# Moving the tiles that TensorE reads to SBUF addresses that are multiples of 512 bytes, in an attention and expert-layer kernel

## The chip, the cores and the metric

The kernel runs on one core of a Trainium2 chip. The metric is device time in microseconds (us), from runs on the chip; a profiled execution has a time of its own beside them, and a span, which is the time from its first instruction to its last.

## What is computed

Eight batches of eight heads. `x` has 512 tokens and `state` 32 rows per head, 64 numbers each. Attention goes both ways between `x` and `state`; the two results are laid one after the other (544 rows in each batch), the heads are joined to rows of 512 numbers, and a layer with a mish activation follows.

```python
scores = scale * np.matmul(x, state.transpose(0, 1, 3, 2))       # 8 x 8 x 512 x 32
a = softmax(scores);   xread = np.matmul(a, state)
scores2 = scale * np.matmul(state, x.transpose(0, 1, 3, 2))      # 8 x 8 x 32 x 512
a2 = softmax(scores2); sread = np.matmul(a2, x)
y = np.concatenate([xread, sread], axis=2)                       # to 4352 x 512
h = y @ w_in                                                     # w_in 512 x 2048
g = h * np.tanh(softplus(h))                                     # mish
out = g @ w_out                                                  # w_out 2048 x 512
```

Weights come as 64-bit floats and are joined to 32-bit ones on the chip; the rest is fp32.

## The kernel before, in words

**Two halves for each factor.** The large products use the type `F32R`. To keep precision, each operand is split in a high and a low part of that type, and each product is three matmuls: high by high, high by low, low by high. So `ah`/`al` are the parts of the attention weights, `swh`/`swl` of state times `w_in`, `gh`/`gl` of the activated hidden layer, and `wo` holds both parts of `w_out`.

**The two big products.** `xread @ w_in` is computed as attention weights times (state times `w_in`): `sw_slice` makes the second factor with small fp32 matmuls into `swp` and splits it. A batch has eight slots; each takes two blocks of 128 hidden columns.

- `gemm1` (the tile `ph`) does 12 matmuls for a slot, each with a weight of 128x128 from `swh` or `swl` and a moving operand of 128x512 from `ah` or `al`. There are 8 batches x 8 slots x 12 = 768.
- `mish` (ScalarE) makes `g` from `ph`; `high_g` and `low_g` (VectorE) split it.
- `gemm2` (the tile `acc`) does 24 matmuls for a slot, each with a weight of 128x128 from `gh` or `gl` and a moving operand of 128x512 from `wo`. There are 8 x 8 x 24 = 1536, and 96 more with the tile `acc_s`.

The 256 rows that come from `state` (`sread`, gathered in `srT_h` and `srT_l`) are multiplied by `w_in` itself in `gemm1_s`, before the last batch: 192 matmuls into `ph_s`, each with a weight of 128x128 from `wh` or `wl` and a moving operand of 128x256 from `srT_h` or `srT_l`.

**Order.** In the first batch each engine's order is written out by hand (the list of steps at L614). After that, the slots run one after another; `gemm2` of a slot comes two slots later (`LAG`), and the attention of the next batch is put beside the slots. All matmuls are issued by helpers, so the profile names one line, L67, for nearly all of them; groups are told apart by their tiles.

**Where tiles lie.** Tiles of a pool are laid one behind the other in each partition of SBUF, in the order in which their tags are first used. The first of the kernel's own is `ident` (L99), at byte 16,512, which is 32 x 512 + 128. It is 512 bytes long, and so are, or multiples of that, all tiles behind it up to the three small softmax tiles `mx`, `s1` and `r1` (L332): 64 bytes each, two buffers of each, 384 bytes in all.

Of the kernel before, what the change touches and what calls it, by code (L numbers as in the profile page):

```python
# [9 lines left out]
F32 = mybir.dt.float32  # L10
# [7 lines left out]
P = 128  # L18
# [56 lines left out]
def state_attention_mish_kernel(ctx, tc, x, state, w_in, w_out, out):  # L75
# [5 lines left out]
    const = ctx.enter_context(tc.tile_pool(name="const", bufs=1))  # L81
    pool = ctx.enter_context(tc.tile_pool(name="pool", bufs=2))
# [4 lines left out]
    def misc(name):  # L87
        return ps_m.tile([P, 512], F32, tag="m", name=name)
# [6 lines left out]
    def temp(name, shape=(P, S)):  # L95
        return pool.tile(list(shape), F32, tag="t", name=name, bufs=5)


    ident = const.tile([P, P], F32, name="ident")  # L99
    make_identity(nc, ident)  # L100

    w_in_sb = const.tile([P, NC, DF], F32, name="w_in_sb")
# [130 lines left out]
    def attention(b, sn, xq=None):  # L233
# [84 lines left out]
        e1, small = {}, {}  # L318

        def wide(a):  # L320
            return a.unsqueeze(2).to_broadcast([P, 16, NS])

        def groups(a):
            return a.rearrange("p (g n) -> p g n", n=NS)

        def transposed(pt, src):
            for t in range(NT):
                last["PE"] = pe.transpose(pt[:, t * P:(t + 1) * P], src[:, t * P:(t + 1) * P], ident)

        def soft1_t(kc):  # L330
            e1[kc] = temp(f"e1_{b}_{kc}")
            small[kc] = [pool.tile([P, 16], F32, tag=n, name=f"{n}_{b}_{kc}") for n in ("mx", "s1", "r1")]  # L332
            if b == 0:
                src = misc(f"scT_{b}_{kc}")
                transposed(src, sc[kc])
            else:
                src = e1[kc]
                dve.transpose(src, sc[kc])
            yield
            mx = small[kc][0]  # L340
            dve.tensor_reduce(mx, groups(src), AX.X, ALU.max)
            dve.tensor_sub(groups(e1[kc]), groups(src), wide(mx))
# [40 lines left out]
        def soft1():  # L383
            whole(*(soft1_t(kc) for kc in two))
            for kc in two:
                soft1_x(kc)
            whole(soft1_n(), *(soft1_a(kc) for kc in two))
# [20 lines left out]
        def sreadT():  # L408
# [8 lines left out]

        own = dict(
            x=x_transposed, st=lambda _: state_blocks(b, sn), sc=lambda _: scores(), tr=soft1_t, ex=soft1_x,
            no=lambda _: soft1_n(), pr=soft1_a, mm=soft2_m, ee=soft2_e, et=e2_transposed, sr=sread,  # L420
            rt=lambda _: sreadT(), fill=fill, aT=aT)
# [229 lines left out]
    for key, j in slots:  # L651
# [15 lines left out]
        n = pending[0][3] // 2  # L667
# [74 lines left out]
```

## Time and profile before

| | us |
|---|---|
| median of 3 runs | 679.45 (678.8 to 679.7) |
| profiled execution, its own time | 678.77 |
| its span | 677.0 |

An engine's busy time is a share of the span. A matmul's duration covers its way through the array, so matmuls that follow each other overlap, and their rate is read from their starts, or from the chain of work that ended last: there the time of a piece is divided by its number of matmuls. "PEld" is the loading of weights, which runs beside matmuls. "PEclk" is the clock that TensorE was granted, in tenths of 2.4 GHz.

### The profile page before, as it was taken

How to read it: one execution, taken by the hardware profiler on the slowest of the kernel's cores; microseconds unless marked ns; L12 is line 12 of the kernel's file. 1: busy time of each engine (PE TensorE's matmuls, PEld its weight loads, DVE VectorE, ACT ScalarE, POOL GpSimd, SP SyncE). 2: the span in 40 equal slices, each digit the busy share in tenths (PEclk: the TensorE clock that was granted, in tenths of full speed). 3: DMA queues.
4: the chain of work that ended last, by engine and by line, in shares of the span. 5: the costliest groups of instructions: out<-in, count | busy, mean ns of one | idle time of the engine just before them, and what ended most of it. 6: DMA issues, size and time to landing. Idle time of an engine off the chain costs nothing.

```text
span 677.0 us, 11013 instructions
## 1 busy us (share of the span) xinstructions
PE 668.7 (99%) x4642; PEld 525.2 (78%) x4642; DVE 339.9 (50%) x520; ACT 263.0 (39%) x418; POOL 0.7 (0%) x6
## 2 busy tenths in 40 slices
PE   8999999999999999999999999999999999999997
PEld 6777777777777777777777877777777789877785
DVE  4878894358328533565327533564427345222221
ACT  4997853245216312541226312632236234122210
POOL 0000000000000000000000000000000000000000
PEclk9999999999999999999999999999999999999999
DMA  9965212401131022302131022202100001000001
GB/s 326 393 232 186 46 19 83 103 7 29 67 74 23 1 63 83 48 1 63 36 74 22 1 63 81 45 0 64 50 14 0 1 1 63 1 17 17 0 1 62
DMA packets 74929, 41.61 MB, mean 61 GB/s; under 512 B 56192, under 2 KB 64384, under 8 KB 74880
## 3 DMA queue, kind: packets, MB, share of 16 engines
q1 hardware_dynamic: 74592, 40.85, 20.6%
q8 instruction: 36, 0.59, 0.4%
q14 instruction: 13, 0.11, 0.0%
q10 hardware_dynamic: 288, 0.07, 0.0%
HBM read 31.98 MB, written 8.91 MB: 60 GB/s over the span
## 4 chain that ended last, share of the span: by engine, by line
PE 90%; DMA 4%; ACT 3%; DVE 2%; issue 1%; SPq 0%; DVEq 0%; ACTq 0%
PE acc L67 51%; PE ph L67 24%; PE swp L67 5%; PE ph_s L67 3%; PE acc_s L67 3%; DMA wir<-in_moe_w_in_dram 2%; PE srp L67 1%; DMA wor<-in_moe_w_out_dram 1%; PE sc L67 1%; ACT L67 1%; PE e2p L67 1%; PE st L67 1%; DVE gl L67 1%; DMA x<-in_x_dram 0%; ACT g L67 0%
## 5 line engine op out<-in xcount | busy, mean ns | idle before, releaser
L67 PE MATMUL acc<-wo,gh 128*128 128x512 f32 x1024 | 326.0, 399 | 0.0
L67 PEld LDWEIGHTS acc<-wo,gh 128*128 128x128 f32 x1024 | 188.8, 188 | 51.8 <-issue 9.8
L67 PE MATMUL acc<-wo,gl 128*128 128x512 f32 x512 | 202.6, 396 | 0.1
L67 ACT ACTIVATE g<-ph 128x512 f32<-128x512 f32 x128 | 74.0, 598 | 210.1 <-DVE gl L67 193.6
L67 PEld LDWEIGHTS acc<-wo,gl 128*128 128x128 f32 x512 | 96.2, 188 | 23.6 <-DVE gl L67 0.8
L67 DVE CAST gh<-g 128x1024 fp32r<-128x1024 f32 x64 | 44.3, 692 | 114.9 <-PE acc L67 106.5
L67 DVE TENSOR_TENSOR swl<-swp,swh 128x512 fp32r<-128x512 f32 (+1 forms) x72 | 43.0, 626 | 95.7 <-ACT swh L67 95.6
L67 DVE TENSOR_TENSOR gl<-g,gh 128x1024 fp32r<-128x1024 f32 x64 | 78.1, 1220 | 4.8 <-DVE gh L67 0.5
L67 PE MATMUL ph<-ah,swh 128*128 128x512 f32 x256 | 79.9, 394 | 0.2 <-ACT g L67 0.2
L67 PE MATMUL ph<-al,swh 128*128 128x512 f32 x256 | 78.9, 390 | 0.0
L67 PE MATMUL ph<-ah,swl 128*128 128x512 f32 x256 | 78.6, 390 | 0.0
L67 PEld LDWEIGHTS ph<-ah,swh 128*128 128x128 f32 x256 | 47.7, 188 | 11.6 <-ACT g L67 0.7
L67 ACT CAST swh<-swp 128x512 fp32r<-128x512 f32 (+1 forms) x72 | 35.3, 546 | 54.0 <-PE swp L67 54.0
L67 PEld LDWEIGHTS ph<-al,swh 128*128 128x128 f32 x256 | 48.1, 188 | 10.5
L67 PEld LDWEIGHTS ph<-ah,swl 128*128 128x128 f32 x256 | 48.1, 188 | 10.3
L67 ACT ACT_TABLE_LOAD x35 | 44.9, 1283 | 16.3 <-DVE sm L67 10.9
L67 PE MATMUL swp<-w_in_sb,bd 64*32 64x256 f32 x1024 | 36.0, 383 | 0.3 <-DVE w_in_sb L67 0.2
L67 DVE STREAM_TRANSPOSE xT<-xq 128x512 f32<-128x512 f32 x24 | 25.5, 1101 | 17.4 <-PE e2p L67 17.3
L67 PEld LDWEIGHTS swp<-w_in_sb,bd 64*32 64x32 f32 x1024 | 15.2, 106 | 16.9 <-issue 12.7
L67 ACT COPY o<-acc 128x512 f32<-128x512 f32 x16 | 9.4, 586 | 48.0 <-PE acc L67 40.4
L67 DVE COPY o<-acc 128x512 f32<-128x512 f32 x16 | 11.1, 691 | 22.6 <-PE acc L67 17.2
L67 PE MATMUL acc_s<-wo,gh_s 128*128 128x512 f32 x64 | 20.2, 396 | 0.0
(76 smaller groups left out, 482.7 us busy)
## 6 DMA issues: line engine op xcount, KB each, us to landing
x<-in_x_dram SPq DMA_DIRECT2D x32, 256.0 KB, 3.9
wir<-in_moe_w_in_dram SPq DMA_DIRECT2D x16, 512.0 KB, 10.1
wor<-in_moe_w_out_dram SPq DMA_DIRECT2D x16, 512.0 KB, 6.9
out_dram<-o SPq DMA_DIRECT2D x32, 256.0 KB, 2.3
xq<-in_x_dram SPq DMA_DIRECT2D x192, 32.0 KB, 2.3
out_dram<-o_s SPq DMA_DIRECT2D x8, 64.0 KB, 1.7
sn<-in_state_dram SPq DMA_DIRECT2D x14, 32.0 KB, 2.0
sn<-in_state_dram ACTq DMA_DIRECT2D x2, 32.0 KB, 3.1
```

Of the source, the lines that this page charges most:

```text
L67: made = method(*args, **kwargs)
```

## The change

```diff
-    ident = const.tile([P, P], F32, name="ident")
+    ident = const.tile([P, 96 + P], F32, name="ident")[:, 96:]
     make_identity(nc, ident)
...
         def soft1_t(kc):
             e1[kc] = temp(f"e1_{b}_{kc}")
-            small[kc] = [pool.tile([P, 16], F32, tag=n, name=f"{n}_{b}_{kc}") for n in ("mx", "s1", "r1")]
+            small[kc] = [
+                pool.tile([P, n], F32, tag=t, name=f"{t}_{b}_{kc}")[:, :16] for t, n in (("mx", 32), ("s1", 16), ("r1", 16))]
```

The identity gets 96 unused floats (384 bytes) in front of it, and each of the two buffers of `mx` gets 64 unused bytes behind its 16 numbers. No instruction is added, removed or moved on any engine: the built programs differ in addresses and line numbers alone. The addresses, from the allocation of the two built programs (a name with several buffers shows the first; their distances are multiples of 512 unless the row says otherwise):

| tile | read by TensorE as | first byte before | past a multiple of 512 | first byte after | past a multiple of 512 |
|---|---|---|---|---|---|
| `ident` | moving, in transposes | 16,512 | 128 | 16,896 | 0 |
| `w_in_sb` | moving of `swp` | 17,024 | 128 | 17,408 | 0 |
| `srT_h`, `srT_l` | moving of `ph_s` | 49,792 | 128 | 50,176 | 0 |
| `wo` (eight tiles) | moving of `acc`, `acc_s` | 57,984 | 128 | 58,368 | 0 |
| `xT`, `e1`, `e2`, `wh`, `wl` (five buffers shared) | `wh`, `wl`: weights of `ph_s` | 149,120 | 128 | 149,504 | 0 |
| `bd` | weights of `swp` (slices 128 bytes apart) | 159,360 | 128 | 159,744 | 0 |
| `mx` | not read | 165,504 | 128 | 165,888 | 0 |
| `ah`, `al` | moving of `ph` | 165,888 | 0 | 166,400 | 0 |
| `swh`, `swl` | weights of `ph` | 182,272 | 0 | 182,784 | 0 |
| `gh`, `gl` | weights of `acc`, `acc_s` | 206,848 | 0 | 207,360 | 0 |
| `srd` | weights of eight transposes | 223,424 | 192 | 223,936 | 192 |

The weights of `ph`, `ph_s`, `acc` and `acc_s` are slices of 512 bytes at multiples of 512 bytes within their tiles. The moving operands of `ph`, `acc` and `acc_s` are 2,048 bytes long, and all begin at a multiple of 2,048 bytes within their tiles; taken by 2,048, `ah` and `al` begin at 0 before and at 512 after, `wo` at 640 before and at 1,024 after.

## Rows read from the trace of the kernel before

**Rows 1.** The page: span, then each engine's busy time; granted clock by slice.
```profile
span 677.0 us, 11013 instructions
...
PE 668.7 (99%) x4642; PEld 525.2 (78%) x4642; DVE 339.9 (50%) x520; ACT 263.0 (39%) x418; POOL 0.7 (0%) x6
...
PEclk9999999999999999999999999999999999999999
```

**Rows 2.** The page: chain that ended last, by engine, then by line.
```profile
PE 90%; DMA 4%; ACT 3%; DVE 2%; issue 1%; SPq 0%; DVEq 0%; ACTq 0%
PE acc L67 51%; PE ph L67 24%; PE swp L67 5%; PE ph_s L67 3%; PE acc_s L67 3%; DMA wir<-in_moe_w_in_dram 2%; PE srp L67 1%; DMA wor<-in_moe_w_out_dram 1%; PE sc L67 1%; ACT L67 1%; PE e2p L67 1%; PE st L67 1%; DVE gl L67 1%; DMA x<-in_x_dram 0%; ACT g L67 0%
```

**Rows 3.** Waits of PE: engine, tile, waited for: us in total, times, longest.
```profile
PE warm L67 <- POOL ident masks.py:199: 1.4, 1, 1.4
PE scT L67 <- ACT scs L67: 0.8, 1, 0.8
...
```

**Rows 4.** Chain that ended last, in order: start us, us, what, number.
```profile
542.73 5.79 PE acc L67 x24
...
551.42 11.50 PE ph_s L67 x96
562.92 5.58 PE acc L67 x24
568.50 5.75 PE ph_s L67 x48
574.25 5.58 PE acc_s L67 x24
...
629.69 5.59 PE acc L67 x24
635.28 2.73 PE ph L67 x12
638.01 2.80 PE acc L67 x12
640.81 1.02 PE swp L67 x32
...
647.57 5.59 PE acc L67 x24
653.17 2.73 PE ph L67 x12
655.90 14.01 PE acc L67 x60
```

**Rows 5.** Busy time of each engine by stretch; then granted clock, DMA share, GB/s.
```profile
23.00:40.00 17.00, 16.64 (x96) 12.60 (x88) 13.55 (x18) 16.90 (x23) 0.00 (x0) 1.00 1.05 388
80.00:100.00 20.00, 19.73 (x124) 14.27 (x123) 19.90 (x34) 11.85 (x19) 0.00 (x0) 1.00 0.17 27
100.00:540.00 440.00, 439.83 (x3100) 343.83 (x3099) 217.00 (x344) 156.27 (x260) 0.00 (x0) 1.00 0.17 42
...
656.00:669.00 13.00, 13.00 (x57) 10.49 (x56) 2.39 (x3) 0.54 (x1) 0.00 (x0) 1.00 0.00 0
```

**Rows 6.** Weight loads by tile: shapes, number, busy us, mean ns of one, idle.
```profile
L67 PEld LDWEIGHTS acc<-wo,gl 128*128 128x128 f32 x512 | 96.2, 188 | 23.6 <-DVE gl L67 0.8
L67 PEld LDWEIGHTS ph<-al,swh 128*128 128x128 f32 x256 | 48.1, 188 | 10.5
...
L67 PEld LDWEIGHTS ph_s<-srT_h,wh 128*128 128x128 f32 x64 | 12.3, 192 | 0.1
```

**Rows 7.** Chain that ended last, its start, same columns.
```profile
0.74 3.07 DMA x<-in_x_dram
...
4.29 7.86 DMA wor<-in_moe_w_out_dram
...
12.16 11.45 DMA wir<-in_moe_w_in_dram
```

## The prediction

> **What bounds the kernel now.** I read first the busy times, then the chain of work that ended last, then who TensorE waited for. TensorE (PE) is busy 99% of the span [rows 1] and holds 90% of the chain [rows 2]. A busy PE could still be a waiting one, so the waits decide: PE waited eight times in the whole execution, once for 1.4 us and once for 0.8 us at the start, and the other six are shorter still [rows 3]. From 100 to 540 us VectorE is busy 217 of 440 us and ScalarE 156, while PE has 439.8 of 440 [rows 5]. So the end is set by how closely matmuls follow each other, and a fraction of a nanosecond per matmul counts, if it holds for hundreds of them. The granted clock is full, 2.4 GHz, in every slice [rows 1], and plays no part.
>
> **At what rate they follow.** In the chain, pieces of one kind of matmul stand with their time and number [rows 4], and the quotient is the spacing:
>
> - `ph`: 2.73 us for 12, 227.5 ns each.
> - `acc`: 5.59 us for 24, 232.9 ns each; the last piece, 14.01 us for 60, gives 233.5 ns. `acc_s` reads the same `wo`: 5.58 for 24, 232.5 ns.
> - `ph_s`, with 256 columns: 11.50 us for 96, 119.8 ns each.
>
> `ph` and `acc` are the same instruction: weights of 128x128, a moving operand of 128x512, both of the same type, six and more of them summed in one bank. Yet `acc` takes 5.4 ns longer each time. It isn't the other engines: in the last piece VectorE is busy 2.39 us of 13 and ScalarE 0.54, no DMA runs [rows 5], and the spacing is the longest of all. What differs is where the operands lie. In `ph` the moving operand (`ah`, `al`) and the weights (`swh`, `swl`) all begin at a multiple of 512 bytes. In `acc` the weights do, and the moving `wo` begins 128 bytes past one.
>
> **What kind of effect it would be.** 512 and 256 columns at 2.4 GHz are 213.3 and 106.7 ns, worked out from the granted clock. So `ph` has 14.2 ns over its columns, `ph_s` 13.1 and `acc` 19.6. `ph_s` has no more than `ph`, although its moving `srT` begins 128 bytes past a multiple of 512. But its weights `wh`, `wl` do so as well. A start that is off for itself would have to show in `ph_s`, at least in part; a start that is off against the other operand would show in `acc` alone, which is what the rows have. While one matmul's 512 columns are read, the weights of the next are read beside them (188 ns of the 233 are weight loading [rows 6]), so two streams out of SBUF run at once and can get in each other's way, or not, by their addresses. There is also a direct sign that starts matter: a weight load takes 188 ns from `gl` and `swh`, which are at a multiple of 512, and 192 ns from `wh`, which is 128 past one, with the same shape [rows 6]. The weights in `ph` and `acc` begin at every multiple of 512, not of 1,024 or 2,048 alone, and the mean of 188 ns leaves no room for a finer rule there.
>
> After the change `wo`, `gh`, `gl`, `ah`, `al`, `swh` and `swl` all begin at multiples of 512: by both readings, absolute and relative, `acc` should have the spacing of `ph`.
>
> **The change part by part.** No instruction is added or moved, so there are only the prices of addresses.
>
> - *`acc` and `acc_s`*, 1536 + 96 = 1632 matmuls. From 232.9 ns to what `ph` has, 227.5 ns, is 5.4 ns. `ph` pieces have heavier company than `acc` (the splitting of `g` on VectorE falls in them), so `acc` may come out a little below; the excess of the last, undisturbed piece over `ph` is 233.5 - 227.5 = 6.0 ns. I take 5.7 ns: 1632 x 5.7 = 9.3 us. With 5.4 it is 8.8, and with 6.0 it is 9.8.
> - *What of it isn't on the path.* The 192 `acc` matmuls of the first batch run beside full engines: ScalarE 16.90 of 17 us from 23 to 40, VectorE 19.90 of 20 from 80 to 100 [rows 5]. There a faster PE meets a later `gl` or `wo`. At most 192 x 5.7 = 1.1 us is lost, at least 0; I take half, 0.55. From 100 us on the other engines are busy half the time, and nothing else is near.
> - *`ph`*, 768 matmuls, moves by 512 bytes and keeps its place by 512. I take 0; the other end is the second rival below.
> - *`ph_s`*, 192 matmuls, weights and moving operand move alike. Its weight loads should go from 192 to 188 ns, which is hidden: the loads overlap each other, since 119.8 ns is shorter than one. I take 0.
> - *The small fp32 matmuls* (`swp` 5% of the chain, `srp`, `sc`, `e2p` 1% each [rows 2], together 8% of 677 us, about 54 us) also get other addresses. A block of `swp` takes 1.02 us for 32 [rows 4]. I take 0, since no row shows one of them at another start; if they changed by the share that `acc` does (5.4 of 232.9, 2.3%), it would be 1.2 us either way.
> - *DMAs, VectorE, ScalarE.* All loads now land at multiples of 512. In the first 24 us they are on the path: 3.07 + 7.86 + 11.45 = 22.4 us [rows 7]. No row shows a load to a multiple of 512, so again 0, bounded by the same 2.3% either way, 0.5 us. VectorE and ScalarE have idle time for what a start may cost them. The setting of `ident` delays nothing: as many bytes are written as before. The Trainium skill (DMA: Bandwidth & Descriptors, "How a descriptor splits into AXI transactions") says that a transfer which doesn't start at a multiple of 256 bytes needs one transaction more; a row of 2,048 bytes at 128 past would take 9 instead of 8. By that page the loads would gain up to a ninth of 22.4 us, 2.5 us as an estimate; no row here shows it.
>
> The sum: 9.3 - 0.55 = 8.75 us less. Against the profiled execution's own time that is 678.77 - 8.75 = 670.0 us; that execution is 0.7 us under the median of the runs, 679.45, and against this it is 670.7 us, the forecast.
>
> **The rivals.**
>
> *Nothing changes, 679.45 us.* The 5.4 ns would then belong to `acc` for another reason: `wo` is read in the order high, low, high, the weight `gh` is used twice in a row, and four banks take turns instead of two. For it speaks that `ph_s`, at 128 past, has as little over its columns as `ph`, so that a plain rule "off a multiple of 512 is slow" is wrong as it stands; against it the 188 and 192 ns, and that I find no mechanism in these three. The Trainium skill also stands on this side: SBUF — State Buffer, "Who interferes with whom", gives TensorE two independent read ports, one for the moving operand and one for weights, and says that it never waits on anyone; by it `acc` and `ph` should run alike already, and the rows (232.9 against 227.5) disagree.
>
> *The boundary of moving operands is 1,024 bytes: 674.8 us.* `wo` then comes right, at 1,024 past a multiple of 2,048, and `ah`, `al`, at 512, go wrong. 768 x 5.4 = 4.1 us come back: 670.7 + 4.1 = 674.8. The trace can't exclude it, because moving `ah` and `al` stand only at multiples of 2,048 in it.
>
> *The boundary is 2,048 bytes: slower, 683.6 us.* The mechanism is the same, and the place is `ph`: `wo` at 1,024 stays as slow as it is, while `ah` and `al` lose the multiple of 2,048 that they had. 679.45 + 4.1 = 683.6. It decides from the point where a moving operand must begin at a multiple of its own length. Against it and the one before: the weights show no difference between multiples of 512, so two streams that meet by their distance can't tell them apart either.
>
> **How the numbers follow.** The forecast, `acc` near `ph`'s spacing, gets 0.76; 1,024 bytes 0.06; nothing 0.11; 2,048 bytes 0.07. Within the forecast, the low end is 9.8 us for `acc` with nothing lost, 1.2 for the small matmuls and 0.5 for the loads: 679.45 - 11.5 = 668.0. Its high end is 8.8 - 1.1 = 7.7 us gained and 1.2 + 0.5 lost elsewhere: 673.5. I widen the range at the top to 676.0, to hold the case of 1,024 bytes, and by half a microsecond at the bottom, to 667.5, since a spacing below that of `ph` can't be excluded; it then holds a little over 0.8. The forecast's own range is 668.0 to 673.5. A measurement of this kernel can tell about 0.2%, 1.4 us, from no change. Faster by more: 0.76 + 0.06 = 0.82; within it 0.11; slower 0.07.
>
> **What would show it.** In the chain of the changed kernel, pieces of 24 `acc` should take 5.4 to 5.5 us instead of 5.59, the last 60 about 13.65 instead of 14.01, and pieces of 12 `ph` still 2.73. `ph_s` stays at 5.75 for 48, with weight loads at 188 instead of 192 ns. If `acc` falls and `ph` rises to 2.80, the boundary is larger than 512. If `acc` falls but the end doesn't follow, waits of PE on VectorE's `gl` will have appeared. If `acc` stays at 232.9, the addresses aren't the reason, and the forecast is wrong at its first step.

## The result: 670.15 us, and the profile after

The changed kernel has a median of 670.15 us (669.92 to 670.25, 4 runs), beside 679.29 us of the kernel before; the ratio is 0.9867, with a 95% interval of 0.9853 to 0.988. The profiled execution took 670.19 us, its span is 668.4 us.

From the page of the changed kernel, span and busy times, as in [rows 1]:

```profile
span 668.4 us, 11013 instructions
...
PE 659.5 (99%) x4642; PEld 525.1 (79%) x4642; DVE 339.1 (51%) x520; ACT 263.0 (39%) x418; POOL 0.7 (0%) x6
```

TensorE (PE) does the same 4642 matmuls in 9.2 us less, and still has 99% of the span. The chain of work that ended last, in order (start us, us, what, number), answers to [rows 4]:

```profile
561.69 5.75 PE ph_s L67 x48
567.44 5.47 PE acc_s L67 x24
...
621.98 5.44 PE acc L67 x24
627.42 2.72 PE ph L67 x12
630.14 2.72 PE acc L67 x12
632.86 1.02 PE swp L67 x32
...
639.55 5.44 PE acc L67 x24
644.99 2.72 PE ph L67 x12
647.71 13.62 PE acc L67 x60
```

24 `acc` matmuls take 5.44 us instead of 5.59, which is 226.7 ns each instead of 232.9; the last 60 take 13.62 us instead of 14.01, 227.0 instead of 233.5. `ph` has 2.72 us for 12, 226.7 ns, so the two products now run alike. `ph_s` and `swp` are as they were.

Summed from start to start over both traces, `acc` and `acc_s` cost 8.1 us less, `ph` 0.9 us less, all the rest 0.4 us more; the last matmul starts 8.7 us earlier.

Almost none of that gain is from the first batch. Two pieces of it in the chain of the kernel before, then a piece and the end of it in that of the changed kernel:

```profile
61.16 1.59 PE acc L67 x6
...
102.78 2.74 PE ph L67 x12
```

```profile
61.16 1.59 PE acc L67 x6
...
87.91 1.14 DVE gl L67
89.04 1.15 DVE wo L67
90.23 1.42 PE acc L67 x5
91.65 1.02 PE swp L67 x32
92.68 4.33 PE acc L67 x18
97.00 2.72 PE ph L67 x12
99.72 2.93 PE acc L67 x12
102.65 2.72 PE ph L67 x12
```

The first matmuls after 90 us follow VectorE's `gl` and `wo`, the short piece of `acc` at 61.16 us takes as long as before, and the `ph` at 102.65 us stood at 102.78 us before: 0.13 us for a whole batch.

### The profile page after: what moved, and what is told of

Read it like the earlier page. It is cut to its first block, busy times and chain, and to the rows that moved or that the text cites. A ratio compares the mean times of both kernels' runs of the same rounds, so it can differ in the third digit from the quotient of the medians.

```text
span 668.4 us, 11013 instructions
## 1 busy us (share of the span) xinstructions
PE 659.5 (99%) x4642; PEld 525.1 (79%) x4642; DVE 339.1 (51%) x520; ACT 263.0 (39%) x418; POOL 0.7 (0%) x6
## 4 chain that ended last, share of the span: by engine, by line
PE 87%; DMA 5%; DVE 4%; ACT 2%; issue 1%; SPq 1%; DVEq 0%; ACTq 0%
PE acc L67 49%; PE ph L67 23%; PE swp L67 4%; PE ph_s L67 3%; PE acc_s L67 3%; DMA wor<-in_moe_w_out_dram 2%; DMA wir<-in_moe_w_in_dram 1%; PE srp L67 1%; DMA x<-in_x_dram 1%; PE sc L67 1%; PE e2p L67 1%; DVE e L67 1%; DVE gl L67 1%; PE st L67 1%; ACT L67 1%
## 5 line engine op out<-in xcount | busy, mean ns | idle before, releaser
L67 PE MATMUL acc<-wo,gh 128*128 128x512 f32 x1024 | 321.2, 395 | 0.2 <-DVE wo L67 0.2
L67 PE MATMUL acc<-wo,gl 128*128 128x512 f32 x512 | 199.9, 390 | 0.1
```

The lines of the kernel that those rows point to most:

```text
L67: made = method(*args, **kwargs)
```

## The experiments

All are the same instructions in the same order, with tiles at other addresses. "At 128" means 128 bytes past a multiple of 512. The theories: A, what counts is the distance between the starts of the moving operand and of the weights; B, the moving operand's own start counts; C, something else.

**All tiles at 128.** The second half of the change alone:

```diff
-    ident = const.tile([P, 96 + P], F32, name="ident")[:, 96:]
+    ident = const.tile([P, P], F32, name="ident")
```

> Only the second half of the change: the small tile is larger, the identity has nothing in front. wo, gh, gl, ah, al, swh, swl, srT, wh, wl then all begin 128 bytes past a multiple of 512. Theory A (what counts is the distance between the starts of the moving operand and of the weights, taken by 512): the distance is 0 everywhere, so acc has 226.7 ns for each matmul, ph too, and the time is that of the changed kernel, 670.2 us, within 1. Theory B (each moving operand must itself begin at a multiple of 512): acc stays at 233 and ph goes from 227.5 to 233, so 679.3 + 768 x 5.4 ns = 683.4 us. Theory C (something else in acc made it slow, and the identity's start or the like cured it): 679 us.

Measured: 670.49 us, ratio to the kernel before 0.9873 (0.9859 to 0.9888), the same as with all tiles at 0. In the chain that ended last:

```profile
622.05 5.44 PE acc L67 x24
627.49 2.72 PE ph L67 x12
...
647.77 13.62 PE acc L67 x60
```

`wo`, `ah` and all their weights are 128 past a multiple of 512, and the pieces of `acc` and `ph` take no longer for it. Theory B falls: none of these tiles has to begin at a multiple of 512, or of 256, for itself.

**The first half alone.** `mx` as before, so `wo` is at 0 and `ah`, `al`, `swh`, `swl`, `gh`, `gl` are at 384:

```diff
-                pool.tile([P, n], F32, tag=t, name=f"{t}_{b}_{kc}")[:, :16] for t, n in (("mx", 32), ("s1", 16), ("r1", 16))]
+                pool.tile([P, n], F32, tag=t, name=f"{t}_{b}_{kc}")[:, :16] for t, n in (("mx", 16), ("s1", 16), ("r1", 16))]
```

> Only the first half of the change: 384 bytes in front of the identity, the small tile as before. wo, srT, wh, wl then begin at a multiple of 512, while ah, al, swh, swl, gh, gl begin 384 bytes past one. Theory A (distance between moving operand and weights): 0 in ph and ph_s, 128 in acc (wo at 0, weights at 384), as in the kernel before, so acc 232.9 ns, ph about 227.5, time 679 us. Theory B (the moving operand's own start): acc 226.7 and ph 233, so 670.2 + 768 x 6 ns = 674.8 us.

Measured: 679.33 us, ratio 1.0001 (0.9991 to 1.001). The chain that ended last:

```profile
630.29 5.59 PE acc L67 x24
635.89 2.73 PE ph L67 x12
...
656.51 14.01 PE acc L67 x60
```

These are the pieces of [rows 4] to the last digit, although every tile lies elsewhere: the distance in `acc` is again 128. Of the two edits, the larger small tile does all of the work, since it brings the distance in `acc` to 0; the bytes in front of the identity, alone, leave the distance in `acc` at 128.

**The distance moved to the other product.** `ah` and `al` alone at 128, all else as in the changed kernel (64 bytes more in each `mx`, and 384 unused bytes behind `al`):

```diff
-... (("mx", 32), ("s1", 16), ("r1", 16))]
+... (("mx", 48), ("s1", 16), ("r1", 16))]
...
             lo = pool.tile([P, S], F32R, tag=f"al{kc}", name=f"al_{b}_{kc}")
+            if b == 0 and kc == 1:
+                pool.tile([P, 96], F32, tag="pad", name="pad", bufs=1)
```

> The changed kernel with ah and al alone (the moving operands of ph) 128 bytes past a multiple of 512; wo and all weights at a multiple of 512. Theory A (distance of moving operand and weights, taken by 256 after the runs with wo at 64 and 256): the slow spacing moves from acc to ph: ph 233 ns (2.80 us for 12), acc 226.7 ns (5.44 us for 24), and 670.2 + 768 x 6.2 ns = 674.9 us. Theory C (the slowness is the wo tile's own, cured by its place): all stays as in the changed kernel, 670 us.

Measured: 675.38 us, ratio 0.9942 (0.9928 to 0.9957). The chain:

```profile
626.96 5.46 PE acc L67 x24
632.41 2.79 PE ph L67 x12
635.21 2.73 PE acc L67 x12
```

Now `ph` is the slow one, 2.79 us for 12 or 232.5 ns, and `acc` runs at 227.5. The slowness goes with the distance, not with the tile, so theory C falls for `wo`, too.

**Other distances of `wo`.** The identity's front and `mx` are sized so that `wo` moves and `ah`, `al` and the weights of both products stay at 0; `srT`, `wh`, `wl` and `w_in_sb` move with `wo` (front, then `mx`, in floats: 32 and 64 for 256 bytes; 112 and 24 for 64; 16 and 72 for 192; 104, 16 and one unused tile of 24 floats in front of `mx` for 32). The first, as a diff against the changed kernel:

```diff
-    ident = const.tile([P, 96 + P], F32, name="ident")[:, 96:]
+    ident = const.tile([P, 32 + P], F32, name="ident")[:, 32:]
...
-... (("mx", 32), ("s1", 16), ("r1", 16))]
+... (("mx", 64), ("s1", 16), ("r1", 16))]
```

> wo, srT, wh, wl, w_in_sb begin 256 bytes past a multiple of 512; ah, al, swh, swl, gh, gl at a multiple of 512. By both theories, a period of 256 bytes would give acc at 226.7 ns and 670 us; with a period of 512 acc stays slow, at 233 ns or more (256 is the farthest that it can be from 0), so 679 us or more: if the extra time grows with the distance, twice 6 ns, 239 ns and 689 us.

Measured: 670.81 us, ratio 0.9876 (0.9861 to 0.989). The chain with `wo` at 256:

```profile
639.58 5.44 PE acc L67 x24
645.02 2.72 PE ph L67 x12
647.74 13.61 PE acc L67 x60
```

A distance of 256 is as good as 0.

> wo, srT, wh, wl, w_in_sb begin 64 bytes past a multiple of 512; ah, al, swh, swl, gh, gl at a multiple of 512. If the extra time grows with the distance: half of that at 128, so 3 ns, acc about 230 ns and 675 us. If every distance that isn't 0 costs the same: 233 ns and 679 us. If only steps of 128 bytes count: 226.7 ns and 670 us. ph 226.7 to 228 in all three.

Measured: 676.43 us, ratio 0.996 (0.9945 to 0.9975). The chain with `wo` at 64:

```profile
645.22 5.51 PE acc L67 x24
650.73 2.77 PE ph L67 x12
653.50 13.77 PE acc L67 x60
```

`acc` has 229.6 ns, half of the extra time at 128, which looked like growth with the distance. But `ph` is slower as well, 2.77 us for 12 or 230.8 ns, with both its operands at 0. None of the three expectations had that.

> wo, srT, wh, wl, w_in_sb at 192 past a multiple of 512, ah, al, swh, swl, gh, gl at a multiple of 512. With a period of 256 this is 64 to the other side. If only the size of the distance counts, as with wo at 64: 676.4 us, acc about 230 ns. If it counts which of the two streams is ahead: another value between 670 and 683 us. If the price grows with the distance up to 256: over 679 us.

Measured: 680.24 us, ratio 1.0014 (1.0005 to 1.0024).

> wo, srT, wh, wl, w_in_sb at 32 past a multiple of 512, the others at a multiple. If the price grows with the distance (0 at 0, 3 ns for acc at 64, 6 at 128): 1.5 ns, acc 228.2 ns, 672.5 to 673 us. If steps of 64 count: 226.7 ns, 670.2 us. If any distance that isn't a multiple of 256 starts the carried phase: about 676 us.

Measured: 680.82 us, ratio 1.0023 (1.0014 to 1.0032). The chain with `wo` at 192, then that with `wo` at 32:

```profile
648.90 5.60 PE acc L67 x24
654.50 2.74 PE ph L67 x12
```

```profile
649.59 5.60 PE acc L67 x24
655.20 2.76 PE ph L67 x12
```

Both have 233.3 ns for `acc`. So the price doesn't grow with the distance, and 64 bytes one way and 192 (64 the other way) differ. All three of my guesses for 32 bytes were too low: its median is the longest of the study.

**Is slowness handed on?** `ah` and `al` at 64, `wo` and all weights at 0 (as the run with 128, with 40 floats in `mx` and 112 behind `al`):

> The same with ah and al 64 bytes past a multiple of 512. In the run with wo at 64 both acc (229.8 ns) and ph (230.4 ns) were slower, although ph's operands were both at 0. Theory A alone: only ph is slower here, by 3 ns: 670.2 + 768 x 3 ns = 672.5 us, acc at 226.7 ns. Theory A with a carried phase (a stretch of matmuls hands its timing of weight loads against streams on to the next one): acc is slower as well, by up to 3 ns: up to 670.2 + 2400 x 3 ns = 677 us.

Measured: 675.38 us, ratio 0.9945 (0.993 to 0.996). The chain:

```profile
644.27 5.49 PE acc L67 x24
649.76 2.76 PE ph L67 x12
```

`ph` has 230.0 ns. `acc`, whose operands are all at 0, has 228.8 ns instead of 226.7. In the starts behind these pieces, the first ten `acc` matmuls after a `ph` stretch take 224 to 236 ns, then they settle at 226 and 227. So a stretch with a bad distance can make the next stretch slow, until that finds its rhythm again. The same is in the kernel before: the first three `ph` matmuls after `acc` take 231, 233 and 230 ns there (the median of 52 stretches behind the first batch), the others 227, and after the change all take 227.

A bad distance isn't needed for such a slow start. In the changed kernel `ph_s` has both starts at 0, and yet the 24 `acc_s` behind it, at 567.44 us in the chain above, take 5.47 us, where 24 `acc` behind `ph` take 5.44: the first five take 228 to 236 ns, the others 226 to 228. Stretches of `acc` behind the small fp32 matmuls begin in the same way. Why a stretch begins slowly isn't shown.

**One weight in three.** `gl` alone at 128, by 128 unused bytes in front of it:

```diff
+        if key == "0_0":
+            pool.tile([P, 32], F32, tag="pad", name="pad", bufs=1)
         gl = pool.tile([P, W], F32R, tag="gl", name=f"gl_{key}")
```

> The changed kernel with gl alone (the weights of every third acc matmul) 128 bytes past a multiple of 512; wo, gh and all of ph at a multiple. Theory A1 (the weights of a matmul get in the way of the operand that is streamed while they are loaded, which is the matmul before): within each three acc matmuls the second gh, during which gl is loaded, takes longer than 226.7 ns, the others don't or by what is carried on. Theory A2 (a matmul and its own weights): the gl matmul itself takes longer. Price by both: a third of the 6.2 ns, 2.1 ns for each acc matmul, 670.2 + 1632 x 2.1 ns = 673.6 us; less if a single distance of 128 between two of 0 is made up for, up to 679 us if its phase is carried on over the next matmuls.

Measured: 676.16 us, ratio 0.9953 (0.9939 to 0.9968). The chain, and then TensorE's matmuls in order of time (start us, us, what, number):

```profile
651.18 2.72 PE ph L67 x12
653.90 13.88 PE acc L67 x60
```

```profile
657.20 0.62 PE L67 MATMUL acc<-wo,gh 128*128 128x512 f32 x2
657.66 0.40 PE L67 MATMUL acc<-wo,gl 128*128 128x512 f32 x1
657.89 0.62 PE L67 MATMUL acc<-wo,gh 128*128 128x512 f32 x2
658.35 0.40 PE L67 MATMUL acc<-wo,gl 128*128 128x512 f32 x1
658.59 0.62 PE L67 MATMUL acc<-wo,gh 128*128 128x512 f32 x2
```

The mean over 60 is 231.3 ns, 4.3 more than in the same piece of the changed kernel (227.0), and not the 2.1 that a third of the price would be. From a start of `gl` to the next `gh` there are 0.23 and 0.24 us, while two `gh` have 0.46. Read to the nanosecond, each three go 227, 232, 234: the first `gh` isn't slower, the second `gh`, during which `gl` is loaded, takes 5 ns longer, and the `gl` matmul itself 7. A1 and A2 both saw one of the two. Here nothing is handed on to `ph`, 2.72 us.

**256 columns.** `srT_h` and `srT_l`, the moving operands of `ph_s`, alone at 128:

```diff
+    const.tile([P, 32], F32, name="pad0")
     srT = [const.tile([P, NC, B * NS], F32R, name=f"srT_{n}") for n in ("h", "l")]
+    const.tile([P, 96], F32, name="pad1")
```

> The changed kernel with srT_h and srT_l alone (the moving operands of ph_s, 256 columns) 128 bytes past a multiple of 512, their weights wh and wl at a multiple. If the distance counts in ph_s as in acc: its spacing rises from 119.9 by 3 to 7 ns, 192 x 5 ns = 1 us, 671.2 us. If 256 columns leave no such cost: 119.9 ns and 670.2 us, and the low spacing of ph_s in the kernel before says nothing about the distance.

Measured: 670.41 us, ratio 0.9871 (0.9854 to 0.9887). The chain:

```profile
544.42 11.52 PE ph_s L67 x96
555.93 5.48 PE acc L67 x24
561.42 5.76 PE ph_s L67 x48
```

120.0 ns each, against 119.8 with the changed kernel's piece above. With 256 columns, a distance of 128 costs nothing that shows in `ph_s` itself. The 24 `acc` behind it begin with ten slow matmuls (224 to 236 ns) where the changed kernel has five, 5.48 us instead of 5.47.

Together, the spacing of matmuls with 512 columns by the distance of their two starts:

| distance, by 256 | product | kernel | ns each, from the chain |
|---|---|---|---|
| 0 | `acc`, `ph` | changed; all at 128; `wo` at 256 | 5.44 / 24 = 226.7 |
| 32 | `acc` | `wo` at 32 | 5.60 / 24 = 233.3 |
| 64 | `acc` | `wo` at 64 | 5.51 / 24 = 229.6 |
| 64 | `ph` | `ah`, `al` at 64 | 2.76 / 12 = 230.0 |
| 128 | `acc` | before; first half alone | 5.59 / 24 = 232.9 |
| 128 | `ph` | `ah`, `al` at 128 | 2.79 / 12 = 232.5 |
| 192 | `acc` | `wo` at 192 | 5.60 / 24 = 233.3 |

## Why the prediction was right, and where its steps were not

**What bounds the kernel: right.** TensorE's longest wait is 1.4 us, at the start, before and after, and the time followed its spacing.

**The first step, the comparison of `acc` with `ph`: right, for the reason called relative.** It's the distance between the two streams: all tiles at 128 are as fast as all at 0, the first half alone is as slow as before, and `ph` becomes slow when its own distance is 128. That two streams of TensorE get in each other's way fits the run with `gl` alone at 128, where the matmul during which the odd weights are loaded is slower; but the one that uses them is, too, and whether they meet in SBUF, and where, isn't shown. No run could take the weight loads away. By the Trainium skill (SBUF — State Buffer, "Who interferes with whom"), the two read ports of TensorE are independent and it never waits on anyone. That gives no reason for a difference between these matmuls, and the measurement decides: 226.7 against 229.6 to 233.3 ns by address alone.

**Two of the rows under it couldn't carry what I put on them.** The weight loads of 188 and 192 ns were called a direct sign that starts matter. After the change `wh` begins at a multiple of 512, and its loads take as long as before, by tile (shapes, number, busy us, mean ns, idle), to hold against [rows 6]:

```profile
L67 PEld LDWEIGHTS acc<-wo,gl 128*128 128x128 f32 x512 | 96.1, 188 | 21.2 <-DVE gl L67 0.9
...
L67 PEld LDWEIGHTS ph_s<-srT_h,wh 128*128 128x128 f32 x64 | 12.3, 192 | 0.1
```

So the 4 ns have another reason, which these runs don't tell. And `ph_s` was called as the witness for the relative reading, because it is quick with both operands at 128. It is as quick with a distance of 128, so it would have looked the same under either reading. The conclusion drawn from it was right, the row didn't support it. What carried the forecast was the comparison of `acc` and `ph` alone.

**The terms.** `acc` and `acc_s` were to give 8.75 us and gave 8.1. Where `acc` follows `ph`, the 5.7 ns for each were too little: such pieces gained 6.2 (232.9 - 226.7) to 6.5 ns (233.5 - 227.0). The reason was a wrong reading of `ph`: its 227.5 ns in the kernel before were not the company of VectorE's splitting, but what `acc` handed on to it. Hence also the term of `ph`, taken as 0, was 0.9 us. Where `acc` follows other products, 5.7 ns were too much, since these stretches begin slowly with all starts at 0, too: 24 `acc_s` behind `ph_s` went from 5.58 to 5.47 us, 4.6 ns each. The prediction had no step for that. The term of the first batch was too kind for the same reason: half of 1.1 us was to be lost, but the batch as a whole ends only 0.13 us earlier. Part of it is lost at the VectorE rows shown above, and part in short pieces like the six `acc` at 61.16 us, 1.59 us in both kernels. The other products cost 0.4 us more, for which the terms were 0. These errors nearly cancel, which is luck: 8.1 + 0.9 - 0.4 = 8.6 us against 8.75. The profiled executions differ by 678.77 - 670.19 = 8.6, the medians by 9.1.

**The small matmuls and `ph_s`: right.** `swp` has 1.02 us for 32, and `ph_s` 5.75 us for 48, as before.

**The loads: 0 on the path, right, but they did become quicker.** Busy times, granted clock, DMA share and GB/s from 5 to 25 and 25 to 37 us, of the kernel before, then of the changed one:

```profile
5.00:25.00 20.00, 18.13 (x174) 13.90 (x175) 15.53 (x25) 14.20 (x21) 0.00 (x0) 1.00 1.03 391
25.00:37.00 12.00, 11.77 (x64) 8.86 (x64) 9.16 (x14) 11.93 (x14) 0.00 (x0) 1.00 1.06 382
```

```profile
5.00:25.00 20.00, 18.12 (x176) 13.97 (x175) 15.41 (x25) 14.05 (x21) 0.00 (x0) 1.00 1.04 403
25.00:37.00 12.00, 11.65 (x64) 8.81 (x64) 9.12 (x14) 11.93 (x14) 0.00 (x0) 1.00 1.06 404
```

391 and 382 GB/s become 403 and 404. ScalarE is busy 11.93 of 12 us from 25 to 37 us in both, and the chain reaches VectorE's next `gl` at 36.51 us before and at 36.65 after, so the end gets nothing of it.

**The rivals.** "Nothing" and both larger boundaries are out: `ah` and `al` at 512 past a multiple of 2,048 run at 226.7 ns, and at 128 past one as well, with all tiles at 128. The slower side exists, but elsewhere than I put it: `wo` at 32 or 192 with its weights at 0 is 0.14 to 0.23% slower than the kernel before.

## What to carry to other kernels

Where matmuls follow each other without a gap and two alike products have different spacing, look at the addresses of the moving operand and of the weights: here, with 512 columns of this type, the spacing was shortest where they began at the same remainder by 256 bytes, and an address for itself didn't count. A small tile in the middle of a pool is enough to shift all that lies behind it, so check the remainders after every change of a tile's size; half of this change, the one small tile, gave all of the gain. Compare products with the same shape in the same trace before explaining a difference by the engines beside them.

## What the runs showed of the hardware that was not expected

- The price isn't monotone: 233.3 ns at 32 bytes, 229.6 at 64, 232.9 at 128, 233.3 at 192, and 226.7 at 0 and 256.
- A stretch of matmuls with a bad distance can make the next stretch slower, though its own operands are well placed: 230.8 ns as the mean of the 12 `ph` after `acc` with `wo` at 64. With `gl` alone at 128 nothing was handed on to `ph`. And `acc_s` behind the 256-column `ph_s` begins with five slow matmuls even with all starts at 0 (5.47 instead of 5.44 us for 24).
- Loads into tiles that begin at a multiple of 256 bytes are quicker by 3 to 6% while the DMA engines are full (403 and 404 GB/s against 391 and 382). The first half alone, which also loads into multiples of 512, has 406 and 405; all tiles at 128 has 388 and 382. All twelve kernels fall into these two groups: 398 to 406 and 403 to 405 where the loads go to multiples of 256, 388 to 395 and 380 to 382 where they don't. That agrees in kind with what the Trainium skill (DMA: Bandwidth & Descriptors, "How a descriptor splits into AXI transactions") says of transfers that don't begin at a multiple of 256 bytes, though that section tells it of reads, and here the written side moved; the estimate of a ninth, worked out from it in the prediction, was too much.
